# Hash bits on four column quarters, placed by way of DRAM, with three buffers for x

## The chip, the cores and the metric

One core of a Trainium2 chip. Its engines are TensorE (PE in the profile, PEld its weight loads), VectorE (DVE), ScalarE (ACT), GpSimd (POOL) and SyncE (SP). The metric is the device time of one execution in microseconds, as a median of several runs. All runs told here are of the fast state.

## The reference

Hash attention for 32 heads, followed by a feed-forward block:

```python
q_bits = (np.einsum('bhsd,dk->bhsk', q, proj) > 0)      # 6 bits a query, the same for keys
q_bucket = np.sum(q_bits * powers, axis=-1)
mask = q_bucket[:, :, :, None] == k_bucket[:, :, None, :]
scores = np.where(mask, scale * q @ k.T, -1e9)
attn = softmax(scores); x = attn @ v                     # 4 x 8 heads, 768 tokens, 64 wide
h = x @ w_in                                             # 3072 tokens, 512 -> 2048
out = (h * erf(softplus(h))) @ w_out
```

## The kernel before

The heads go in 16 pairs, the two heads of a pair (a, b) on partitions 0 to 63 and 64 to 127. The mask comes from a matmul of hash bits (qb, kb; values of plus and minus one, the keys weighted by 2^100) that is added to the score matmul in the same bank. The hash of a pair takes four matmuls of 64 columns, in two rounds, and one sign on ScalarE; VectorE then spreads the key bits of each head and doubles the query bits:

```python
def hash_bits(d, big, halves=(0, 1)):
    ...
    for half in halves:
        for n, what in enumerate("qk"):
            nc.tensor.matmul(out=d["bits"][n * D : n * D + D, half, 0:HS], lhsT=proj_sb,
                             rhs=d[what][:, half * HS : (half + 1) * HS], start=True, stop=True)
...
def spread_bits(d, cols, ab):      # twice a pair, 64 x 768
    nc.vector.tensor_scalar(out=d["kb"][ab * D : ab * D + D, cols], in0=d["qb"][D:P, cols],
                            scalar1=weight[D:P, ab : ab + 1], scalar2=None, op0=ALU.mult)
def double_bits(d, cols):          # once a pair, 64 x 768
    nc.vector.tensor_copy(out=d["qb"][D:P, cols], in_=d["qb"][0:D, cols])
```

The result of a pair (x) leaves its PSUM bank (the memory that TensorE writes into) by a ScalarE copy. The divisors (z) go to DRAM and back to be inverted, come back as r, VectorE normalises x and SyncE sends it to DRAM (xs). x has two buffers; z and r take turns in two others:

```python
def home(i, what):
    if i < NPAIR - 1:
        return xst.tile([P, S], F32, name=what, tag="x" if what == "x" else "z")   # bufs=2
```

A list scheduler orders all operations by assumed costs when the kernel is built; every engine then runs its own list strictly in order. TensorE's order is fixed by hand. With h counting half pairs:

```python
order += [("score", n) for n in (2 * h + 1, 2 * h + 2) if n < NS]
if h % 2 == 0 and h // 2 + 1 < NPAIR:
    order.append(("bits", h // 2 + 1))
if h >= 1:
    order.append(("divisor", h - 1))
order += [("weigh", 2 * h), ("weigh", 2 * h + 1)]     # the av groups of the profile
...
op(start_pair, (i,), "SP", 3.6, (0, n - 6),            # loads q, k, v of pair i
   (("weigh", n - 9), ("bits_of", i - 1)) + ..., late=3.5)
```

## Time and profile before

| | before |
|---|---|
| time, median of 4 runs | 933.61 us |
| attention with setup, in the profiled run | 339.4 us |
| feed-forward part | 593.5 us |
| one pair of heads, undisturbed | 20.32 us |
| busy in such a period: PE, VectorE, ScalarE | 20.32, 19.64, 15.86 us |
| PE stalls over 14 pairs | 4.3 us |

The first two stretches and the period are shown in the prediction. In this program the useful yardstick is the start of each av group (24 passes, once per half pair): the distances between them show every stall, which the share of busy time does not, because PE is marked busy nearly throughout. I call the 32 groups av 0 to av 31.

### The profile page before, as it was taken

Reading aid. Unit: us, or ns where it says so; the run is one execution under the profiler, and the core shown is the slowest. Engines: PE = TensorE matmul, PEld = TensorE weight load, DVE = VectorE, ACT = ScalarE, POOL = GpSimd, SP = SyncE. Lnnn points to the kernel's source line nnn. Section 1 sums busy time; section 2 is a strip of 40 time slices with the busy share of each in tenths; the row PEclk is TensorE's granted clock in tenths of the full one; section 3 lists DMA queues with packets and bytes.
Section 4 is the critical chain, followed back from the end, with each engine's and each line's share of the span. In section 5 each row is a group of like instructions: output and inputs, shape, how many; then the busy total and the mean of one; then the engine's idle time right before and its main releaser. Section 6 shows DMA issues by size and latency. Waiting matters only on the chain.

```text
span 932.9 us, 12993 instructions
## 1 busy us (share of the span) xinstructions
PE 916.8 (98%) x5003; PEld 661.9 (71%) x5003; DVE 829.7 (89%) x1041; ACT 771.0 (83%) x1002; POOL 17.4 (2%) x35
## 2 busy tenths in 40 slices
PE   8999999999999999999999999999999999999996
PEld 3444444444444458888888888888888888888885
DVE  4999998999888997899999889998899789988995
ACT  5888787768876838999998998899989997899891
POOL 0000000000000000000000000000000000000000
PEclk9999999999999999999999999999999999999998
DMA  8365455576654322010212012210221111001211
GB/s 198 99 158 147 132 148 139 147 200 165 147 149 131 97 103 97 1 46 34 80 68 79 34 46 69 80 34 34 79 78 36 34 65 49 34 34 46 68 35 48
DMA packets 61398, 80.92 MB, mean 87 GB/s; under 512 B 33296, under 2 KB 46224, under 8 KB 61328
## 3 DMA queue, kind: packets, MB, share of 16 engines
q1 hardware_dynamic: 56672, 64.08, 23.9%
q0 software_dynamic: 4352, 15.73, 5.6%
q8 instruction: 41, 0.67, 0.3%
q10 hardware_dynamic: 304, 0.20, 0.1%
q14 instruction: 29, 0.24, 0.1%
HBM read 64.07 MB, written 15.93 MB: 86 GB/s over the span
## 4 chain that ended last, share of the span: by engine, by line
PE 85%; DVE 7%; DMA 4%; ACT 2%; issue 1%; SPq 0%; DVEq 0%; ACTq 0%
PE M L1238 30%; PE X L1098 27%; PE st L529 11%; PE av L602 9%; PE M L1098 3%; PE bits L358 2%; DMA xs<-x 1%; ACT e_all L543 1%; DVE x_sum L590 1%; PE z_ps L635 1%; DVE x L590 1%; DMA zd<-z 1%; DMA zc<-zd 1%; DVE x L721 1%; DMA r<-rd 1%
## 5 line engine op out<-in xcount | busy, mean ns | idle before, releaser
L1165 DVE SCALAR_TENSOR_TENSOR e<-w,e 128x1024 f32<-128x1024 f32 x144 | 173.4, 1221 | 5.8 <-ACT w L1161 3.0
L1161 ACT ACTIVATE w<-w,cq 128x1024 f32<-128x1024 f32 x144 | 160.7, 1143 | 1.9
L543 ACT ACTIVATE e_all<-st 128x768 f32<-128x768 f32 x192 | 149.1, 819 | 11.3 <-PE st L529 11.3
L529 PE MATMUL st<-q,k 64*128 64x384 f32 x768 | 156.6, 486 | 0.0
L1238 PE MATMUL M<-w_out_sb,h 128*128 128x256 f32 x576 | 140.2, 380 | 0.4 <-DVE h L1180 0.4
L602 PE MATMUL av<-e_all,v 128*64 128x385 f32 (+1 forms) x768 | 131.1, 490 | 0.0
L1098 PE MATMUL X<-x,w_in_sb 128*128 128x256 f32 x512 | 121.2, 380 | 0.0
L1238 PEld LDWEIGHTS M<-w_out_sb,h 128*128 128x128 f32 x576 | 109.3, 190 | 15.9 <-DVE h L1180 1.1
L1098 PEld LDWEIGHTS X<-x,w_in_sb 128*128 128x128 f32 x512 | 97.1, 190 | 13.8 <-ACT h L1116 0.6
L602 PEld LDWEIGHTS av<-e_all,v 128*64 128x64 f32 x768 | 52.4, 136 | 67.2 <-issue 65.4
L1238 PE MATMUL M<-wt,S 128*128 128x256 f32 x384 | 93.4, 379 | 0.4 <-DVE S L1195 0.4
L529 PEld LDWEIGHTS st<-q,k 64*128 64x128 f32 x768 | 69.1, 190 | 32.8 <-issue 32.1
L1098 PE MATMUL X<-x_sum,w_sum 128*128 128x256 f32 x344 | 81.7, 380 | 1.8 <-ACT h L1116 1.8
L1238 PEld LDWEIGHTS M<-wt,S 128*128 128x128 f32 x384 | 72.9, 190 | 10.7 <-DVE S L1195 0.8
L1098 PEld LDWEIGHTS X<-x_sum,w_sum 128*128 128x128 f32 x344 | 65.1, 190 | 12.0 <-ACT h L1116 3.3
L1116 ACT COPY h<-X 128x512 f32<-128x512 f32 x85 | 49.0, 577 | 22.3 <-PE X L1098 21.4
L1142 DVE SCALAR_TENSOR_TENSOR w<-w,e 128x1024 f32<-128x1024 f32 x48 | 58.4, 1221 | 9.6 <-ACT w L1137 9.3
L529 PE MATMUL st<-qb,kb 64*128 64x384 bf16 x384 | 63.7, 327 | 3.3 <-ACT e_all L543 3.2
L1180 DVE TENSOR_TENSOR h<-h,e 128x1024 f32<-128x1024 f32 x48 | 58.0, 1221 | 6.1 <-ACT e L1176 5.9
L659 ACT COPY x<-av 128x384 f32<-128x384 f32 x32 | 15.3, 478 | 57.4 <-DMA xs<-x 28.8
L1156 ACT ACTIVATE w<-e 128x1024 f32<-128x1024 f32 x48 | 50.4, 1050 | 13.3 <-DVE e L1152 13.0
L1152 DVE TENSOR_TENSOR e<-e,w 128x1024 f32<-128x1024 f32 x48 | 57.5, 1219 | 2.7 <-ACT e L1148 2.6
(117 smaller groups left out, 1421.0 us busy)
## 6 DMA issues: line engine op xcount, KB each, us to landing
wt<-wt SPq DMA_DIRECT2D x24, 768.0 KB, 4.3
raw<-in_w_out_dram POOLq DMA_DIRECT2D x16, 512.0 KB, 3.9
raw<-in_w_in_dram POOLq DMA_DIRECT2D x14, 512.0 KB, 4.2
v<-in_v_dram SPq DMA_DIRECT2D x32, 192.0 KB, 4.5
xs<-x SPq DMA_DIRECT2D x16, 384.0 KB, 2.4
q<-in_qkT_dram SPq DMA_DIRECT2D x30, 192.0 KB, 3.4
k<-in_qkT_dram SPq DMA_DIRECT2D x30, 192.0 KB, 4.2
r<-rd SPq DMA_DIRECT2D x30, 192.0 KB, 3.5
```

Source lines behind the costliest of these rows:

```text
L529: nc.tensor.matmul(out=st[:, ab, 0:HS], lhsT=d["k" + src][rows, keys], rhs=d["q" + src][rows, cols], start=(part == 0), stop=(part == 1),)
L543: nc.scalar.activation(out=e[:, :, 0:HS], in_=st[:, :, 0:HS], func=AF.Exp, scale=scale)
L602: nc.tensor.matmul(out=d["av"][rows, 0:w], lhsT=d["v"][:, g * GC + c, rows], rhs=e[:, ab, 0:w], start=(g == 0 and c == 0), stop=(g == 1 an ...
L1098: nc.tensor.matmul(out=d[where][:, u, :], lhsT=a[:, kc, f : f + P], rhs=b[:, kc, :], start=(first and u == 0 and kc == 0), stop=(last and ...
L1116: nc.scalar.copy(out=quarter(p, q), in_=st[p][where])
L1142: nc.vector.scalar_tensor_tensor(out=w, in0=w, scalar=-1.0, in1=st[p]["e", v], op0=ALU.add, op1=ALU.subtract)
L1152: nc.vector.tensor_tensor(out=s, in0=s, in1=st[p].pop(("w", v)), op=ALU.subtract)
L1156: nc.scalar.activation(out=z, in_=st[p]["s", v], func=AF.Square)
L1161: nc.scalar.activation(out=q, in_=z, func=AF.Square, bias=cq[:, j : j + 1])
L1165: nc.vector.scalar_tensor_tensor(out=s, in0=st[p].pop(("q", v, j)), scalar=ERF_Q[j][1], in1=s, op0=ALU.add, op1=ALU.mult,)
L1180: nc.vector.tensor_tensor(out=h, in0=h, in1=st[p].pop(("s", v)), op=ALU.mult)
L1238: nc.tensor.matmul(out=banks[name][:, sub, :], lhsT=a[:, u, sub * P : (sub + 1) * P], rhs=b[:, u, :], start=(c == 0 and k == 0), stop=(c = ...
```

## The change

It means to shorten the hash on TensorE by putting its four parts side by side on four column quarters. The bits then lie in other rows than the mask matmul reads. VectorE could move them, in eight instructions a pair (dve_place below); here GpSimd writes them to DRAM and reads them back into place: one write, two reads. VectorE keeps one spread of 64x384. As this takes longer, the hash of a pair moves half a pair earlier in TensorE's order (pair 1 stays). Further, x gets three buffers, z one of its own and r two; the last two sums move into other tiles to make room.

```diff
+                for n, what in enumerate("qk"):
+                    for half in range(2):
+                        row = (2 * n + half) * QR
+                        nc.tensor.matmul(out=d["bits"][row : row + QR, 0, 0:HS], lhsT=proj_q,
+                            rhs=d[what][:, half * HS : (half + 1) * HS], start=True, stop=True)
...
+            def leave_bits(i):
+                bd = pairs[i]["bd"] = dram.tile([4, 2, QB, HS], BF16, name="bd", tag="bd")
+                nc.gpsimd.dma_start(out=bd.rearrange("n a r c -> (n a r) c"), in_=sg)
+            def place_bits(i):
...
+                for ab in range(2):
+                    nc.gpsimd.dma_start(
+                        out=both[i % 2][ab * D : ab * D + NBIT + 1, :, :].rearrange(
+                            "r w (h c) -> r (w h) c", h=2),
+                        in_=bd[:, ab, 0 : NBIT + 1, :].rearrange("n r c -> r n c"))
...
-                if h % 2 == 0 and h // 2 + 1 < NPAIR:
-                    order.append(("bits", h // 2 + 1))
+                if h == 0:
+                    order.insert(3, ("bits", 1))
+                if h % 2 and (h + 3) // 2 < NPAIR:
+                    order.append(("bits", (h + 3) // 2))
...
-                    return xst.tile([P, S], F32, name=what, tag="x" if what == "x" else "z")
+                    shape, bufs = {"x": (S, 3), "z": (HS, 1), "r": (S, 2)}[what]
+                    return xst.tile([P, shape], F32, name=what, tag=what, bufs=bufs)
```

(Cut: the constants for the quarters, the clearing of the bit tiles, the new homes of the last sums, and the scheduler's dependencies and costs.)

More of the change, by code (lines that the diff above doesn't have):

```diff
@@ L230 @@
     QR = 32
+    QB = QR // 2
     WARM = 7
@@ L233 @@
     weight = const.tile([P, 2], F32, name="weight")
+    proj_q = const.tile([P, QR], F32, name="proj_q")
+    weight_q = const.tile([P, 1], F32, name="weight_q")
     ones = const.tile([P, D], F32, name="ones")
@@ L257 @@
     nc.gpsimd.dma_start(out=row, in_=bucket)
-    steps = const.tile([P, 5], F32, name="steps")
+    steps = const.tile([P, 8], F32, name="steps")
     for c, (end, factor) in enumerate(
@@ L265 @@
             (QR + NBIT + 1, -float(NBIT)),
+            (QB, -1.0),
+            (QB + NBIT, NBIT + 1.0),
+            (QB + NBIT + 1, -float(NBIT)),
         )
@@ L277 @@
     nc.vector.reduce_sum(out=weight[:, 1:2], in_=steps[:, 2:5], axis=AX.X)
+    nc.vector.memset(proj_q, 0.0)
+    for ab in range(2):
+        rows = slice(ab * D, ab * D + D)
+        nc.vector.tensor_copy(
+            out=proj_q[rows, ab * QB : ab * QB + NBIT],
+            in_=proj_in[rows, ab * NBIT : (ab + 1) * NBIT],
+        )
+    nc.vector.reduce_sum(out=weight_q, in_=steps[:, 5:8], axis=AX.X)
+    nc.vector.tensor_tensor(out=weight_q, in0=weight_q, in1=weight[:, 0:1], op=ALU.add)
+    nc.vector.tensor_copy(out=weight_q[D + QR : P, :], in_=weight_q[D : D + QR, :])
     nc.vector.memset(sgn, -(2.0**-27))
@@ L364, in hash_bits, with sign_bits @@
                 )
-    def sign_bits(d, bitp, cols):
+    def sign_bits(d, tile_of, cols):
         if cols.start == 0:
             for what in ("qb", "kb"):
-                d[what] = bitp.tile([P, S], BF16, name=what, tag=what)
+                d[what] = tile_of(what)
         nc.scalar.activation(
@@ L392, in double_bits, with take_bits @@
         nc.vector.tensor_copy(out=d["qb"][D:P, cols], in_=d["qb"][0:D, cols])
-    def take_bits(d, bitp, halves=(0, 1)):
+    def take_bits(d, tile_of, halves=(0, 1)):
         cols = slice(halves[0] * HS, (halves[-1] + 1) * HS)
-        sign_bits(d, bitp, cols)
+        sign_bits(d, tile_of, cols)
         for ab in (1, 0):
@@ L404, in attention @@
             tc.tile_pool(name="load", bufs=3) as load,
-            tc.tile_pool(name="bitp", bufs=2) as bitp,
+            tc.tile_pool(name="bitp", bufs=1) as bitp,
             tc.tile_pool(name="ep", bufs=1) as ep,
-            tc.tile_pool(name="sums", bufs=2) as sums,
-            tc.tile_pool(name="xst", bufs=2) as xst,
+            tc.tile_pool(name="xst", bufs=1) as xst,
             tc.tile_pool(name="rawp", bufs=2) as rawp,
@@ L415, in big @@
                 return psum.tile([P, 2, 512], F32, name=name, tag="big", bufs=3)
+            sg = bitp.tile([P, HS], BF16, name="sg")
+            both = [bitp.tile([P, 2, S], BF16, name=f"both{n}") for n in range(2)]
+            nc.gpsimd.memset(both[1], 0.0)
             junk = ep.tile([P, HS], BF16, name="junk")
@@ L574, in sum_keys @@
                     if h >= NH - 2:
-                        d["sum", half] = sums.tile([P, 1, 2, HS], F32, name="sum", tag="sum")
+                        if half:
+                            room = blocks[1][:, :, :].rearrange("p k t -> p (k t)")[:, 0:S]
+                        else:
+                            room = load.tile([P, S], F32, name="q", tag="q")
+                        d["sum", half] = room.rearrange("p (n a c) -> p n a c", n=1, a=2)
                     else:
@@ L612, in home @@
                 if i < NPAIR - 1:
-                    return xst.tile([P, S], F32, name=what, tag="x" if what == "x" else "z")
+                    shape, bufs = {"x": (S, 3), "z": (HS, 1), "r": (S, 2)}[what]
+                    return xst.tile([P, shape], F32, name=what, tag=what, bufs=bufs)
                 rows = blocks[1][:, :, :].rearrange("p k t -> p (k t)")
-                return rows[:, S : 2 * S] if what == "x" else rows[:, 0:S]
+                c = {"x": S, "z": 2 * S, "r": 0}[what]
+                return rows[:, c : c + (HS if what == "z" else S)]
             def measure(i, n, half):
@@ L757, in attention @@
                 hash_bits(pairs[0], big, (half,))
-                take_bits(pairs[0], bitp, (half,))
+                take_bits(pairs[0], lambda what: both[0][:, "qk".index(what[0]), :], (half,))
             NH = NPAIR * 2
@@ L773, in bits_of, with weigh_bits, clean @@
             def bits_of(i):
-                hash_bits(pairs[i], big)
-            def sign_of(i):
-                sign_bits(pairs[i], bitp, slice(0, S))
-            def weigh_bits(i, ab):
-                spread_bits(pairs[i], slice(0, S), ab)
-            def copy_bits(i):
-                double_bits(pairs[i], slice(0, S))
+                d = pairs[i]
+                d["bits"] = big("bits")
+                for n, what in enumerate("qk"):
+                    for half in range(2):
+                        row = (2 * n + half) * QR
+                        nc.tensor.matmul(
+                            out=d["bits"][row : row + QR, 0, 0:HS],
+                            lhsT=proj_q,
+                            rhs=d[what][:, half * HS : (half + 1) * HS],
+                            start=True,
+                            stop=True,
+                        )
+            def sign_of(i):
+                nc.scalar.activation(
+                    out=sg,
+                    in_=pairs[i].pop("bits")[:, 0, 0:HS],
+                    func=AF.Sign,
+                    scale=2.0**100,
+                    bias=sgn[:, 0:1],
+                )
+            def weigh_bits(i):
+                nc.vector.tensor_scalar(
+                    out=sg[D:P, :],
+                    in0=sg[D:P, :],
+                    scalar1=weight_q[D:P, 0:1],
+                    scalar2=None,
+                    op0=ALU.mult,
+                )
+            def leave_bits(i):
+                bd = pairs[i]["bd"] = dram.tile([4, 2, QB, HS], BF16, name="bd", tag="bd")
+                nc.gpsimd.dma_start(out=bd.rearrange("n a r c -> (n a r) c"), in_=sg)
+            def place_bits(i):
+                d = pairs[i]
+                bd = d.pop("bd")
+                for n, what in enumerate(("qb", "kb")):
+                    d[what] = both[i % 2][:, n, :]
+                for ab in range(2):
+                    nc.gpsimd.dma_start(
+                        out=both[i % 2][ab * D : ab * D + NBIT + 1, :, :].rearrange(
+                            "r w (h c) -> r (w h) c", h=2
+                        ),
+                        in_=bd[:, ab, 0 : NBIT + 1, :].rearrange("n r c -> r n c"),
+                    )
+            def clean():
+                nc.gpsimd.memset(both[0], 0.0)
             chain = []
@@ L797, in attention @@
                     i = n // 4
-                    after = tuple(("weigh_bits", i, ab) for ab in range(2)) + (("copy_bits", i),)
+                    after = (("place_bits", i),)
                     for c in range(GC):
@@ L803, in attention @@
                 elif what == "bits":
-                    pe(bits_of, (n,), 1.34, (("start_pair", n), slots[-3]))
+                    pe(bits_of, (n,), 0.92, (("start_pair", n), slots[-3]))
                     slots.append(("sign_of", n))
@@ L837, in attention @@
                         after += (("divisor", h - 2),)
+                        if h == NH - 2:
+                            after += (("measure", NPAIR - 3, 0, 1),)
                     op(sum_keys, (h, k), "DVE", 1.72 if where == 2 else 0.92, (1, 2 * h + 1, k), after)
@@ L846, in attention @@
                     (0, 2 * h, -1),
-                    (("divisor", h), ("send", i - 1) if i == NPAIR - 1 else ("widen", i - 1)),
+                    (("divisor", h), ("spread", i - 1)),
                 )
@@ L866, in attention @@
                     )
-                    op(sign_of, (i,), "ACT", 0.88, (0, n - 2, 9), (("bits_of", i), ("score", n - 5, 2)))
-                    for ab in (1, 0):
-                        op(weigh_bits, (i, ab), "DVE", 0.43, (0, n - 2, 1), (("sign_of", i),))
+                    op(sign_of, (i,), "ACT", 0.6, (0, n - 6, 9), (("bits_of", i), ("leave_bits", i - 1)))
+                    op(weigh_bits, (i,), "DVE", 0.33, (0, n - 6, 1), (("sign_of", i),))
+                    op(leave_bits, (i,), "POOL", 0.7, (0, n - 6, 2), (("weigh_bits", i),), late=2.6)
                     op(
-                        copy_bits,
+                        place_bits,
                         (i,),
-                        "DVE",
-                        0.35,
-                        (0, n - 2, 2),
-                        (("weigh_bits", i, 0), ("weigh_bits", i, 1)),
+                        "POOL",
+                        1.2,
+                        (0, n - 6, 3),
+                        (("leave_bits", i), ("score", n - 5, 2)) + (("clean",),) * (i == 2),
+                        late=2.6,
                     )
@@ L899, in attention @@
                     (0, n, 3),
-                    (("ungather", i), ("send", i - 1)),
+                    (("ungather", i), ("normalise", i - 2)),
                     late=6.5,
@@ L904, in attention @@
                 op(send, (i,), "SP", 0.35, (0, n, 4), (("normalise", i),), late=2.2)
+            op(clean, (), "POOL", 1.4, (0, 0), (("score", 3, 2),), late=0.3)
             for n in range(len(pieces)):
@@ L973, in general @@
                 hash_bits(d, big)
-                take_bits(d, bitp)
+                take_bits(d, lambda what: bitp.tile([P, S], BF16, name=what, tag=what))
                 x = ep.tile([P, S], F32, name="x", tag="x")
```

## The prediction

> **What bounds the kernel now.** I read the page's engine line and the 40 slices first, then a three-stretch table of busy time, then the chain of waits, then the timeline of the attention stretch.
>
> ```profile
> PE 916.8 (98%) x5003; PEld 661.9 (71%) x5003; DVE 829.7 (89%) x1041; ACT 771.0 (83%) x1002; POOL 17.4 (2%) x35
> ...
> PE 85%; DVE 7%; DMA 4%; ACT 2%; issue 1%; SPq 0%; DVEq 0%; ACTq 0%
> ```
> The first line says TensorE (PE) is nearly always occupied, the second that 85% of the chain that ended last is its work. A busy PE is not proof of a PE bound, so I asked how the time splits:
>
> ```profile
> 9.60:339.40 329.80, 325.96 (x2290) 150.69 (x2289) 300.17 (x419) 256.07 (x463) 16.55 (x30) 1.00 0.54 142
> 339.40:932.90 593.50, 583.63 (x2700) 509.86 (x2700) 527.06 (x602) 513.03 (x538) 0.00 (x0) 1.00 0.16 55
> ```
> Columns: length, then busy us of PE, PEld, DVE, ACT, POOL, then clock, DMA share, GB/s. Attention takes 330 us, the feed-forward part 594 us. The change edits attention and its setup only, so I expect the 594 us to stay, and everything is decided in the first stretch. There one pair of heads repeats every 20.32 us (the z_ps group at 101 us to the av group at 121.66 us, below). What PE does at the end of such a period:
>
> ```profile
> 119.02 0.81 PE L529 MATMUL st<-q,k 64*128 64x384 f32 x4
> 119.76 0.54 PE L358 MATMUL bits<-q,proj_sb 128*64 128x384 f32 x1
> 119.76 0.54 PE L358 MATMUL bits<-k,proj_sb 128*64 128x384 f32 x1
> 120.13 0.49 PE L358 MATMUL bits<-q,proj_sb 128*64 128x384 f32 x1
> ...
> 121.20 0.53 PE L635 MATMUL z_ps<-x,ones 128*32 128x192 f32 x8
> 121.66 3.78 PE L602 MATMUL av<-e_all,v 128*64 128x385 f32 x22
> ```
> Columns: start, duration, engine, line, names, shape. Every fp32 matmul shows as two passes. Start to start is the cost, since the ends overlap. A q pass and a k pass start together (they sit on two column halves of the array) and the next two come 0.32 us later: four steps of 0.32 plus 0.16 of changeover, 1.44 us for the hash bits. The divisor (z_ps) puts four 32-column matmuls on four column quarters, and all eight passes of 192 columns take 0.46 us: two steps of 0.16 plus 0.14. Four quarters do run side by side here.
>
> PE is not quite gapless. From the av group at 29.56 us to that at 318.32 us in the chain are 14 pairs, 288.76 us; 14 x 20.32 = 284.48. So 4.3 us are stalls. Where:
>
> ```profile
> 286.97 0.73 ACT L460 ACTIVATE keep<-keep,tiny 128x512 int32<-128x512 f32 x1
> 293.69 0.48 ACT L659 COPY x<-av 128x384 f32<-128x384 f32 x1 [5.99 <-DMA xs<-x]
> 294.07 2.22 ACT L543 ACTIVATE e_all<-st 128x768 f32<-128x768 f32 x3
> ```
> ```profile
> 292.14 0.81 PE L529 MATMUL st<-q,k 64*128 64x384 f32 x4
> 294.94 0.34 PE L529 MATMUL st<-qb,kb 64*128 64x384 bf16 x2 [1.99 <-ACT e_all L543]
> ```
> ScalarE wants to empty the av bank into x, whose buffer is still being sent out; it sits 5.99 us, its exponentials behind it come late, and PE waits 1.99 us for a score bank. The table of waits has this kind seven times, 28.8 us of ACT time, longest 6.0.
>
> **What the Trainium skill says.** "TensorEngine Tiling (Array Packing)", section "Key Properties": tiles execute in parallel, and changing the tiling mode drains the array; section "Available Configurations" lists 128x32 as four tiles. The trace agrees: four at once, and some 0.10 to 0.16 us at each change of shape. "DMA: Bandwidth & Descriptors", section "Anatomy of one DMA": a GpSimd-issued transfer costs about 2.0 us plus bytes/436e3, mostly the receipt of the last byte. The trace's only small one, the 0.5 KB row load, landed in 2.9 us; the 512 KB weight loads took 3.9 to 4.2. The same page, "Rules for kernel authors": a transfer that reads what another wrote must wait for its semaphore, so the trip by way of DRAM costs two landings in a row. "SBUF — State Buffer", section "Who interferes with whom": GpSimd and a VectorE operation in a two-port mode lock each other out. In this trace 30 GpSimd issues beside a VectorE that is over 90% busy took 0.53 to 0.77 us, so I expect no starvation.
>
> **The change part by part.**
> 1. Hash matmuls: four of 64 columns in two rounds become four of 32 columns in one round. Two steps of 0.32 plus 0.16 is 0.80 us, or 0.70 if the changeover to the divisor, which now has the same tiling, disappears. Saved: 0.64 to 0.74 us, on the PE path, for 15 pairs (pair 0 keeps the old way). I take 0.69: **-10.4 us**.
> 2. VectorE loses two spreads of 0.419 and a copy of 0.354 (1.19 us a pair), and gains one 64x384 spread of 0.318: -0.87 us a pair. ScalarE's sign shrinks from 0.901 (128x768) to 0.580 (128x384): -0.32. Both lie beside PE, so no direct gain; but VectorE is busy 19.64 of 20.32 us in the period from 101.41 to 121.73 us, and without this relief a PE period of 19.63 us would just meet it. With it, VectorE needs 18.8.
> 3. Three x buffers: the copy out of the av bank waits for a send one pair older, which in the trace ended some 20 us earlier than the one waited for; the longest wait is 6. All seven waits should go. I count most of the stalls as recovered: **-3.6 of 4.3 us**.
> 4. Own divisor buffer: z and r took turns in two buffers, so z already waited only for its own spread. Two for r let the broadcast come earlier. Worth nothing directly.
> 5. The DRAM trip: sign 0.6, spread 0.3, write 0.7 to issue and in all about 2.9 to land, two reads of about 0.7 and then 2.9: roughly 9 us with queueing. From pair 2 on the bits are computed half a pair earlier, and between them and the first score that needs them lie two av groups (8.06), two divisors (0.9) and nine scores (7.4): 16 us. Hidden. Pair 1 cannot be moved earlier: between its bits (end about 19.5 us) and its first score lie one av group (4.03) and three scores (2.43), so PE is there at 25.9. The chain is sign to 20.9, spread to 21.3, write landed 24.2, reads issued to 25.6, landed about 27.9. A stall once: **+2.0 us**.
> 6. Setup: some ten small VectorE instructions of 0.06 to 0.17 us and two GpSimd memsets. VectorE's setup ended at 4.80 us, PE's first hash matmul came at 5.78 behind the warm-up: **+0.3 us** at most.
>
> Sum: -10.4 - 3.6 + 2.0 + 0.3 = -11.7; 933.7 becomes 922.0.
>
> **Rivals.**
> - The trip takes the place of the removed work: GpSimd's queue is in order and its weight loads wait for free buffers (up to 25 us in the table of waits). If a load that waits for VectorE stands ahead of the placing, PE stalls in many pairs. Against: 16 us of slack against 9, and the loads fire about once per half pair, just before the hash. If wrong, 1 to 2 us in half of the pairs: 930 to 936.
> - The inputs come too late: hash bits half a pair earlier need q and k 10 us earlier, and the SyncE queue issues them behind a send that waits for VectorE. In the old trace such a load was issued at 268.68 us, behind the send at 268.27. Against: the load's place in the queue followed the previous pair's hash, which moves forward too. If it stays behind the sends, up to 1 us a pair comes back: 925 to 932.
> - ACT or DVE becomes the bound at 19.63 us a pair: DVE would be at 95%, as now (97%), so bursts might cost some of part 1: 925.
> - No overlap of the quarters: gain of part 1 gone, 932. The divisor speaks against it.
> - Everything recovers and pair 1 has no stall: 918.
>
> **Range and chances.** The terms of part 1 are seen in the trace, to within 1.5 us in sum; the stalls and pair 1 are good to 2 us each; the rivals mostly push up. Range 917.5 to 928. Over 2% faster would need below 915, more than all savings together allow; 2% slower needs a new stall in every pair.
>
> **What would show it.** Hash groups of 128*32 shape, 120 passes, start to start about 0.7 us from bits to z_ps; a period of about 19.6 us; no ACT copy of x that waits for xs<-x; one PE wait for placed bits near 26 us and none later; the feed-forward stretch within 1 us of 593.5. Repeated PE waits on GpSimd's transfers, or hash matmuls that wait for q or k, would prove me wrong.

## The result, and the profile after

| | before | after |
|---|---|---|
| median | 933.61 us (931.88 to 935.03, 4 runs) | 920.59 us (918.86 to 923.69, 4 runs) |
| ratio of the fast runs | | 0.9865, 95% interval 0.9832 to 0.9899 |

A ratio here is the mean time of one kernel's fast runs over that of the other's in the same rounds, so it is not quite the ratio of the medians. The change saves 13.0 us by the medians, 1.35% by the ratio: within 2%.

The page of the kernel after, its engine line and the first line of its chain of waits:

```profile
PE 904.2 (99%) x5003; PEld 657.1 (72%) x5003; DVE 820.2 (89%) x1020; ACT 768.2 (84%) x1002; POOL 46.1 (5%) x82
...
PE 95%; DVE 2%; ACT 1%; DMA 1%; issue 0%; POOL 0%; DVEq 0%; POOLq 0%
```

PE is busy 12.6 us less with the same 5003 passes, and its share of the chain has gone from 85% to 95%: the DMA and VectorE pieces of the chain, 11% together before, are 3%. The two long stretches, in the columns told in the prediction:

```profile
9.60:325.10 315.50, 313.38 (x2289) 146.03 (x2288) 289.95 (x391) 253.46 (x463) 43.85 (x76) 1.00 0.59 156
325.10:917.70 592.60, 583.64 (x2700) 509.71 (x2700) 526.18 (x600) 512.92 (x537) 0.00 (x0) 1.00 0.16 54
```

The attention stretch is 14.3 us shorter, the feed-forward part 0.9. The end of a period on PE, in the timeline:

```profile
107.50 0.81 PE L547 MATMUL st<-q,k 64*128 64x384 f32 x4
108.24 0.52 PE L805 MATMUL bits<-q,proj_q 128*32 128x384 f32 x2
108.25 0.52 PE L805 MATMUL bits<-k,proj_q 128*32 128x384 f32 x2
108.59 0.49 PE L805 MATMUL bits<-q,proj_q 128*32 128x384 f32 x2
108.60 0.49 PE L805 MATMUL bits<-k,proj_q 128*32 128x384 f32 x2
108.91 0.51 PE L659 MATMUL z_ps<-x_sum,ones 128*32 128x192 f32 x8
109.35 4.09 PE L624 MATMUL av<-e_all,v 128*64 128x384 f32 x24
```

Four passes start within 0.01 us of each other and the next four about 0.33 us later. From the first hash pass to the divisor it is 0.67 us where it was 1.44. The period is 19.53 us in place of 20.32.

The two profiled runs, cut at the starts of the av groups:

| piece | before | after | difference |
|---|---|---|---|
| start to av 0 | 20.09 | 18.90 | -1.19 |
| av 0 to av 1 | 9.39 | 11.56 | +2.17 |
| av 1 to av 29 | 288.77 | 273.54 | -15.23 |
| av 29 to the first feed-forward matmul | 21.13 | 21.13 | 0.00 |
| from there to the end | 593.52 | 592.57 | -0.95 |
| whole span | 932.90 | 917.70 | -15.20 |

Four later runs with the new hash order have no stall between av 1 and av 29 and take 272.77 us there; two of them have none between av 0 and av 1 and take 10.09 us. With these I split the 15.2 us:

- the shorter hash: 0.56 for pair 1 (1.34 to 0.78 us up to av 0), and (284.48 - 272.77) - (10.09 - 9.39) = 11.0 for the rest, in all **-11.6 us**;
- stalls between av 1 and av 29: from 288.77 - 284.48 = 4.3 to 273.54 - 272.77 = 0.8, **-3.5 us**;
- a new stall between av 0 and av 1: 11.56 - 10.09, **+1.5 us**;
- start and end: -0.6 and -0.95 us, which I do not ascribe to the change. The start is told below; the end varies by such an amount between all the runs here.

The profiled run of before (934.86 us) was 1.2 us above its median and that of after (919.47 us) 1.1 below, which is why the traces differ by more than the medians.

The new stall, in the timeline of the kernel after (all engines, the rows that concern pair 1):

```profile
19.10 0.60 ACT L814 ACTIVATE sg<-bits,sgn 128x384 bf16<-128x384 f32 x1
...
19.74 0.32 DVE L824 TENSOR_SCALAR sg<-sg,weight_q 64x384 bf16<-64x384 bf16 x1
...
20.36 0.55 POOL L834 DMA_DIRECT2D bd<-sg  x1 [17.05 <-DVE sg L824]
...
24.05 1.14 POOL L843 DMA_DIRECT2D both<-bd  x2 [3.14 <-DMA bd<-sg]
...
26.27 0.32 PE L547 MATMUL st<-both 64*128 64x384 bf16 x1 [0.74 <-DMA both<-bd]
...
26.83 0.33 PE L547 MATMUL st<-both 64*128 64x384 bf16 x1 [0.24 <-DMA both<-bd]
```

This is the chain of the prediction: sign, spread, write, wait for the write, two reads, and PE waits for each of the two. The stall of 0.8 us between av 1 and av 29 is of another kind, at 66 us:

```profile
64.08 0.69 ACT L471 ACTIVATE keep<-raw 128x512 f32<-128x512 f32 x1 [3.98 <-DMA raw<-in_w_in_dram]
...
66.65 0.34 PE L547 MATMUL st<-both 64*128 64x384 bf16 x2 [0.59 <-ACT e_all L561]
```

GpSimd's weight load came late, behind a placing (GpSimd had sat 4.18 us before the placing at 56.98 us), ScalarE waited for the weights with the exponentials behind it, and PE ran out of score banks.

### The profile page after: what moved, and what is told of

The parts are those of the page before. It is cut to its first block, busy times and chain, and to the rows that moved or that the text cites. A ratio compares the mean times of both kernels' runs of the same rounds, so it can differ in the third digit from the quotient of the medians.

```text
span 917.7 us, 13114 instructions
## 1 busy us (share of the span) xinstructions
PE 904.2 (99%) x5003; PEld 657.1 (72%) x5003; DVE 820.2 (89%) x1020; ACT 768.2 (84%) x1002; POOL 46.1 (5%) x82
## 4 chain that ended last, share of the span: by engine, by line
PE 95%; DVE 2%; ACT 1%; DMA 1%; issue 0%; POOL 0%; DVEq 0%; POOLq 0%
PE M L1313 31%; PE X L1173 28%; PE st L547 16%; PE av L624 14%; PE M L1173 3%; PE z_ps L659 1%; PE bits L805 1%; ACT e_all L561 1%; PE warm L773 0%; DVE e L1227 0%; PE bits L374 0%; DMA bd<-sg 0%; DVE h L1255 0%; DMA both<-bd 0%; DVE S L1270 0%
## 5 line engine op out<-in xcount | busy, mean ns | idle before, releaser
L561 ACT ACTIVATE e_all<-st 128x768 f32<-128x768 f32 x192 | 151.5, 813 | 14.2 <-PE st L547 12.8
L547 PE MATMUL st<-both 64*128 64x384 bf16 x384 | 63.7, 326 | 1.6 <-DMA both<-bd 1.0
L1195 DVE TENSOR_TENSOR h<-X,h 128x512 f32<-128x512 f32 x65 | 44.8, 689 | 16.4 <-PE X L1173 15.4
```

What stands on the lines that cost most here:

```text
L547: nc.tensor.matmul(out=st[:, ab, 0:HS], lhsT=d["k" + src][rows, keys], rhs=d["q" + src][rows, cols], start=(part == 0), stop=(part == 1),)
L561: nc.scalar.activation(out=e[:, :, 0:HS], in_=st[:, :, 0:HS], func=AF.Exp, scale=scale)
```

## The experiments

Theory A is that of the prediction: PE is the bound of attention, the hash gain is on its path in full, the third x buffer removes the stalls, the DRAM trip is hidden except for pair 1. Theory B, formed on reading the trace of after: the stalls went because the earlier hash lets the scheduler put a pair's input loads ahead of the send of x on SyncE. In the kernel before, SyncE does this (its timeline; SPq marks a transfer that SyncE issues):

```profile
81.95 0.33 SPq L727 DMA_DIRECT2D xs<-x  x1
82.37 1.13 SPq L342 DMA_DIRECT2D q<-in_qkT_dram  x2
83.55 1.23 SPq L342 DMA_DIRECT2D k<-in_qkT_dram  x2
84.82 1.17 SPq L347 DMA_DIRECT2D v<-in_v_dram  x2
86.09 0.58 SPq L678 DMA_DIRECT2D zd<-z  x1
```

and in the kernel after this:

```profile
94.19 1.18 SPq L358 DMA_DIRECT2D q<-in_qkT_dram  x2
95.42 1.23 SPq L358 DMA_DIRECT2D k<-in_qkT_dram  x2
96.74 1.12 SPq L363 DMA_DIRECT2D v<-in_v_dram  x2
98.88 0.34 SPq L751 DMA_DIRECT2D xs<-x  x1
99.74 0.59 SPq L702 DMA_DIRECT2D zd<-z  x1
```

Before, the send stands first and has waited for VectorE (so in all periods but one: the loads at 96.05 us stand ahead of their send), then come the loads, and only then the divisor's spread (zd), which the next send depends on: 5.1 us after the av group at 81.01 us. After, the loads stand in the time in which the send would wait anyway; in the period before the one shown, the spread was issued 0.5 us after av 6 at 79.73 us (at 80.21 us).

### two_x: the changed kernel with two x buffers

```diff
-                    shape, bufs = {"x": (S, 3), "z": (HS, 1), "r": (S, 2)}[what]
+                    shape, bufs = {"x": (S, 2), "z": (HS, 1), "r": (S, 2)}[what]
```

> The changed kernel with two x buffers in place of three, all else kept. Theory A (the one of the prediction: the third x buffer took the stalls away): the copies out of the av bank wait for the send again, some seven waits of up to 6 us on ScalarE, TensorE loses about 3.5 us, time about 924. Theory B (the hash half a pair earlier lets the input loads stand ahead of the sends in the SyncE queue, so the sends end earlier: in the changed trace a send is issued at 98.88 us and the copy that two buffers would hold back comes at 103.4): waits of under 1 us each, TensorE loses under 1 us, time 920 to 921.5.

Measured: 923.82 us (922.5 to 925.85, 4 runs), ratio 0.9909 to the kernel before. ScalarE waits for the send three times, 12.2 us in all. From av 1 to av 29 it is 275.35 us, so 2.6 us of stalls: between the two theories. The rest of its time is at the start, for another reason. Its scores were at full rate before 9.8 us (12.2 us in the trace of after), so the hash of pair 1 came 1.75 us earlier; its bits did not (the write took 4.6 us to land in place of 3.0, and the reads were issued at 23.99 us, against 24.05), so PE waited 3.6 us, and then ran slowly. Windows of this run, in the columns of before, the clock third from the right:

```profile
20.00:24.00 4.00, 3.78 (x26) 1.56 (x22) 2.60 (x6) 2.70 (x5) 0.01 (x1) 1.00 0.38 71
27.00:30.90 3.90, 3.44 (x13) 2.15 (x15) 1.47 (x2) 0.81 (x1) 0.02 (x1) 0.60 0.86 236
```

After the wait the granted clock is 0.60 in this window. From av 0 to av 1 it took 15.93 us in place of 10.09. The Trainium skill, "TensorE: Matmul & The Clock Gate", section "What's actually happening", has PE at half clock after an idle window of about 3.4 us and the windows free-running; the wait of 3.6 us and the varying start agree with both. The interval of this run's ratio (0.9873 to 0.9946) overlaps that of after (0.9832 to 0.9899), so what the missing buffer costs is read from the trace and not from the times.

### bufs_only: the kernel before with the buffers alone

```diff
-                    return xst.tile([P, S], F32, name=what, tag="x" if what == "x" else "z")
+                    shape, bufs = {"x": (S, 3), "z": (HS, 1), "r": (S, 2)}[what]
+                    return xst.tile([P, shape], F32, name=what, tag=what, bufs=bufs)
```

(and the new homes and dependencies of the last sums, z and r, as in the change)

> The kernel before with the buffers alone changed (three for x, an own one for z, two for r, no pool for the last sums) and the hash as it was. If a third x buffer cures the stalls by itself: no ScalarE wait for a send, 14 periods of 20.32 us without the 4.3 us of stalls, time about 930. If the buffers do nothing without the earlier hash: 933 to 934, with the waits still there.

Measured: 932.23 us (20 runs) beside 932.07, ratio 0.9996, interval 0.9982 to 1.001: no gain, and a time between the two that were expected. The waits for the send are gone, as theory A says, yet the stalls from av 1 to av 29 went only from 4.3 to 2.9 us (287.41 us). In its table of waits stands one in their place:

```profile
ACT z L653 <- DMA zd<-z: 5.7, 6, 1.8
```

ScalarE now waits for the z buffer to be read by its spread, which is late behind the loads, and in places PE waits for the key bits from VectorE. One wait was replaced by the next in the same chain.

### loads_first: the kernel before with the loads ahead of the send

```diff
-                        (("weigh", n - 9), ("bits_of", i - 1))
+                        (("weigh", n - 9),)
```

This touches only what the scheduler believes about the loads; real dependencies are kept.

> The kernel before, old hash and two x buffers, only that on SyncE the input loads of a pair stand ahead of the send of x in place of behind it (the order that the changed kernel got from its earlier hash). Theory B: the loads then fill the time in which the send waits for VectorE, the divisor's spread is issued right after the send, some 4 us earlier, and the sends come 3 to 4 us earlier: ScalarE's waits for a send fall from 28.8 us to under 10, the stalls of TensorE over 14 pairs from 4.3 to under 2 us, time 929 to 931.5 against 932 to 933.6. If the buffer count decides: waits and stalls as before, 932 to 934.

Measured: 930.03 us (22 runs) beside 931.36, ratio 0.9984, interval 0.9974 to 0.9993. The wait for the send, in the table of waits of the kernel before, and then in that of this run (total, times, longest):

```profile
ACT x L659 <- DMA xs<-x: 28.8, 7, 6.0
...
ACT x L659 <- DMA xs<-x: 9.7, 3, 3.5
```

The stalls from av 1 to av 29 are 285.27 - 284.48 = 0.8 us, with two buffers and the old hash. So in this trace the kernel whose loads stand ahead of the send is nearly free of the stalls that I had put down to the want of a third buffer. The gain by the median, 1.3 us, is less than the 3.5 us between the traces; the profiled run of before may have had more stalls than a usual one, which I have not shown. The scheduler also moved operations of VectorE and ScalarE in this kernel (TensorE's and GpSimd's lists are the same), so the isolation is not perfect.

### hash_twice: the hash matmuls made twice

```diff
-                for n, what in enumerate("qk"):
-                    for half in range(2):
+                for n, what, half in [(n, w, h) for _ in range(2) for n, w in enumerate("qk") for h in range(2)]:
+                    if True:
```

> The changed kernel with the hash matmuls of pairs 1 to 15 made twice, the second over the first (the same result). If the four-quarter hash lies on the path at its full length: two more steps of 0.32 to 0.33 us a pair, a period of 20.18 us in place of 19.53, 15 times 0.65 is 9.8 us more, about 930.4. If TensorE has slack that hides it: under 3 us more.

Measured: 928.45 us (20 runs), 7.9 more than after; the period is 20.17 us, so 0.64 us more a pair. The hash lies on the path in full. That the sum is 7.9 and not 15 times 0.64 = 9.6 us fits its first groups: av 0 to av 1 took 10.95 us, less than the 12.2 that the doubled hash and the stall of pair 1 would add up to, since the longer PE work may hide part of the wait; the wait also differs between executions (0.7 us in after_again, 1.5 in after).

### more_dve: VectorE gets its relief back

```diff
+                for _ in range(3):
+                    nc.vector.tensor_scalar(
+                        out=idle, in0=idle, scalar1=1.0, scalar2=None, op0=ALU.mult
+                    )
```

> The changed kernel with three idle VectorE instructions of 64x384 bf16 after each pair's spread, some 0.96 us a pair, about what the change took from VectorE (0.87). If VectorE's relief is needed for the period of 19.53 us (18.8 busy now, 19.7 then): a period of about 19.7 us and stalls, 2 to 8 us more, 923 to 929. If the relief is worth nothing on the path: within 1 us of 920.6.

Measured: 924.34 us (922.75 to 925.18, 4 runs), ratio 0.9909: 3.8 us more than after, though the intervals of the ratios (0.9878 to 0.994, 0.9832 to 0.9899) overlap. The period without stalls stays 19.53 us, but there are 276.37 - 272.77 = 3.6 us of them, most in one kind of its table of waits:

```profile
PE av L626 <- DVE ev L691: 2.9, 4, 1.3
```

PE waits for a tiny VectorE instruction that frees the av bank and stands behind other work in VectorE's list. VectorE's share of the chain that ended last is 14% on this run's page and 2% on that of after. So the 0.87 us a pair taken from VectorE is worth some 4 us on the path, by one trace, although the period without stalls does not show it.

### dve_place: VectorE places the bits, no DRAM

```diff
-                nc.vector.tensor_scalar(out=sg[D:P, :], in0=sg[D:P, :], scalar1=weight_q[D:P, 0:1], ...)
+                for half in range(2):
+                    for ab in range(2):
+                        nc.vector.tensor_copy(out=d["qb"][rows, cols], in_=sg[half * QR : (half + 1) * QR, :])
+                        nc.vector.tensor_scalar(out=d["kb"][rows, cols], in0=sg[at : at + QR, :],
+                            scalar1=weight_w[at : at + QR, ab : ab + 1], scalar2=None, op0=ALU.mult)
```

(rows of 32 with zero weights for the other head; the three transfers removed)

> The changed kernel with the bits placed by VectorE in place of the trip by way of DRAM: eight instructions of 32x384 bf16 a pair in place of one of 64x384. Each about 0.25 to 0.32 us, 2.3 us a pair in place of 0.32, so VectorE needs 18.8 + 2.0 = 20.8 us a pair. If VectorE then bounds the pair: a period of 20.5 to 21 us, 933 to 942. If TensorE stays the bound because VectorE's low-rank weight work slips into the feed-forward stretch: 921 to 925.

Measured: 938.93 us (7 runs), ratio 1.0066: 18.3 us more than after, in the range of the first theory. The mechanism is both at once: 282.40 - 272.77 = 9.6 us of stalls from av 1 to av 29 (20.17 us a pair, less than the 20.5 expected), and a wait of 8.1 us in the first feed-forward tile, for VectorE work that had been pushed back (timeline):

```profile
345.31 6.22 PE L1163 MATMUL M<-x_sum,w_sum 128*128 128x256 f32 x16 [8.08 <-DVE x_sum L349]
```

This is what the trip by way of DRAM buys.

### late_bits: the hash back at its old place

```diff
-                if h == 0:
-                    order.insert(3, ("bits", 1))
-                if h % 2 and (h + 3) // 2 < NPAIR:
-                    order.append(("bits", (h + 3) // 2))
+                if h % 2 == 0 and h // 2 + 1 < NPAIR:
+                    order.append(("bits", h // 2 + 1))
```

> The changed kernel with the hash of pair i back at its old place in TensorE's order, half a pair later. Between the hash and the first score that needs it there are then about 6.5 us in place of 16 to 17. If the trip of about 15 us that the changed trace shows (hash at 108.24 us, placed at about 124 us) is what the earlier place hides: TensorE stalls in every pair, by 3 us if the trip shrinks to 9 as the prediction had it, by 8 if it stays at 15: 45 to 120 us more, 965 to 1040. If the trip is short when it is urgent: under 15 us more.

Measured: 943.11 and 951.33 us, two runs that lie 8 us apart (ratio 1.0151, interval 1.0086 to 1.0216), some 27 us more than after; from av 1 to av 29 it is 298.51 us in the first, so about 1.8 us of stall a pair. Both numbers of the expectation missed. The kind of wait is the expected one (15.1 of the 25.7 us as the table counts them, by ends of matmuls that are modelled):

```profile
PE st L547 <- DMA both<-bd: 15.1, 20, 3.0
```

The trip is shorter here than in the kernel after. There VectorE takes the spread 4.1 us after the hash (median of 15) and the reads are issued 9.1 us after it (4.9 to 13.9); here it is 2.4 and about 6 us. The scheduler orders VectorE by what it believes urgent, so the trip of after had spent part of its slack in VectorE's list. The landings are shorter too: 2.3 us for a write and 2.1 for a read in the median, against 3.4 and 4.0 in after. From the hash to the landing of the second read it is 8.8 us in the median here and 14.2 in after. One read of each, first after (landed in 4.9 us) and then this run (2.1 us), in the columns of before, the DMA share second from the right:

```profile
96.97:101.91 4.94, 4.94 (x40) 2.17 (x38) 4.80 (x5) 3.94 (x7) 1.72 (x3) 1.00 1.16 224
...
106.67:108.82 2.15, 2.15 (x16) 0.90 (x12) 2.08 (x5) 1.71 (x3) 1.81 (x4) 1.00 0.07 20
```

VectorE is busy in both lines; what differs is the share of the DMA engines that other transfers keep busy (it can pass 1 where packets overlap). In after the reads fall beside the loads that SyncE issues, in this run mostly not.

### sync_trip: the transfers issued from SyncE

```diff
-                nc.gpsimd.dma_start(out=bd.rearrange("n a r c -> (n a r) c"), in_=sg)
+                nc.sync.dma_start(out=bd.rearrange("n a r c -> (n a r) c"), in_=sg)
```

(the two reads likewise, and the engine of both operations in the scheduler)

> The changed kernel with the three transfers of a pair issued from SyncE in place of GpSimd. Landings should be shorter (the old trace has 1.4 to 2.4 us for small SyncE transfers against 3.4 and 4.0 for these), so the stall of pair 1 should shrink from 1.5 to about 0.5 us. Against it, the queue is in order and already holds loads, sends and the divisor's trip: if these get in each other's way, sends or loads come late and TensorE stalls: 922 to 930. If not: 919.5.

Measured: 940.32 us (934.79 to 943.06, 13 runs), ratio 1.0066, worse than both theories had it. From av 1 to av 29 it is 292.73 us. PE waits six times for k to be loaded (2.9 us) and six times for VectorE's av instruction (6.6 us). I read this as one queue that carries too many waits, which no further run tested; on GpSimd's queue only weight loads stand beside the three transfers.

### early_first: the hash of pair 1 one score group earlier

```diff
-                    order.insert(3, ("bits", 1))
+                    order.insert(2, ("bits", 1))
```

> The changed kernel with the hash of pair 1 one score group earlier (before the third group in place of after it), 2.4 us more for its trip. Theory: the one stall at 26 us goes, from the first av group to the second it takes about 10.05 us in place of 11.56, time 1.5 us lower, about 919. Rival: the inputs of pair 1 are not there yet or the score banks run short, and TensorE waits before the hash in place of after it: no gain.

Measured: 918.75 us (918.42 to 919.32, 4 runs), ratio 0.9854 (0.9821 to 0.9886), which does not part it from after. PE's wait moved forward, as the rival said: 0.7 us before av 0 for the score bank that the sign had not freed, since three of ScalarE's squares stood ahead of the sign. From av 0 to av 1 it is still 10.85 us.

### after_again, first_here, first_here_two_x: pair 1 placed by VectorE

after_again is the changed kernel unaltered. first_here gives pair 1 the eight VectorE instructions of dve_place and clears its tile before pair 3 uses it; first_here_two_x has two x buffers besides.

```diff
-                    after = (("place_bits", i),)
+                    after = (("place_bits" if i != 1 else "place_here", i),)
...
-                        (("leave_bits", i), ("score", n - 5, 2)) + (("clean",),) * (i == 2),
+                        (("leave_bits", i), ("score", n - 5, 2)) + (("clean", i % 2),) * (i in (2, 3)),
```

(place_here is the loop shown under dve_place; first_here_two_x adds the edit of two_x)

> The changed kernel once more, to stand beside the next two on one chip. 919 to 923; its runs should differ by about 2 us among themselves, because the moment when the first matmuls come to full speed differs between executions (at about 13.4 us in the trace of before, 12.2 in that of after, before 9.8 in two_x).

> The changed kernel, only that the bits of pair 1 are placed by VectorE (eight instructions of 32x384, once) and not by way of DRAM. Theory: the trip of pair 1 is the one stall that the change added; without it the time from the first av group to the second is about 10.1 us in place of 11.56 (15.93 in two_x, where TensorE was at full speed earlier, waited 3.6 us and then ran slowly for a while): 1.5 to 4 us less than after_again, 917 to 919.5. Rival: the stall comes back at pair 2 or 3, whose placing now waits for one more memset: no gain.

> first_here with two x buffers. If the third buffer matters also with the earlier hash: ScalarE waits for a send again (3 times, 12.2 us in two_x), TensorE loses 2 to 3 us after the second av group, so 2 to 3 us more than first_here. If the stalls of two_x were its slow start alone: the same as first_here.

| | median | runs | ratio to before | av 0 to av 1 | av 1 to av 29 |
|---|---|---|---|---|---|
| after_again | 920.39 us | 918.2 to 921.21 | 0.9871 | 10.77 | 272.77 |
| first_here | 918.12 us | 917.52 to 919.22 | 0.9846 | 10.09 | 272.77 |
| first_here_two_x | 919.83 us | 919.6 to 920.25 | 0.9863 | 10.09 | 272.77 |

The runs of after_again lie 3.0 us apart, where about 2 were expected. first_here has no PE stall left up to av 31 and the lowest median, by 2.3 us against after_again on the same chip; with 5 and 4 runs the intervals of the ratios (0.9826 to 0.9865, 0.9847 to 0.9894) still overlap. With two x buffers ScalarE waits for a send once, 2.5 us, and PE does not stall at all in the profiled run. Its runs are nevertheless 1.7 us slower than first_here's; the trace shows 0.7 of it before av 1 and 1.4 us after the attention part, which the buffers do not explain. So the third buffer's own worth beside the earlier hash lies between 0 (this trace) and 2.6 us (two_x), by execution.

## Why the prediction was right

The time, 920.59 us, lies in the range, and the saving of 13.0 us is near the forecast 11.7. The signs that it named came true in the trace of after: a period of 19.53 us, 0.67 us from the bits to z_ps, no copy of x that waits for a send, waits for placed bits only near 26 us, a feed-forward stretch of 592.6 us. Two of its readings were loose: the step from the first hash passes to the next is 0.37 us in the lines shown and only the later ones are 0.32, and the 20.32 us run from one av group to another (101.34 to 121.66 us), not from a z_ps group. By its own steps:

1. **Hash matmuls.** Predicted 0.64 to 0.74 us a pair, measured 0.79 in the period. The mechanism was right and hash_twice shows it on the path in full; the term was undersized, 10.4 against 11.6 us. I had taken the middle between a new hash with a changeover (0.80 us) and one without (0.70); it takes 0.67 us, two steps of about 0.33 and nothing else.
2. **VectorE and ScalarE.** "No direct gain, but without it VectorE would just meet the period" held by and large: VectorE is busy 18.20 us in the period from 109.42 to 128.95 us (18.8 were expected), and more_dve lost 3.8 us when it got the work back.
3. **Three x buffers.** Here the size was right by luck and the cause that I gave was only a part. Predicted -3.6 us, and 3.5 us of stalls are gone between the two traces (a usual run of before may have fewer, see loads_first); but bufs_only recovers nothing in time, with 2.9 us of stalls left, and loads_first has them at 0.8 us with two buffers. The step that failed is "all seven waits should go" taken as the recovery of the stalls: the waits went with the buffers, the stalls did not. The loads' place on SyncE, which I had brought up only as a danger, is the other part; each of the two shortens the same chain. How the 3.5 us divide between them in the kernel after is not settled: with the loads ahead, the third buffer was worth 2.6 us in the trace of two_x and nothing in that of first_here_two_x.
4. **Own divisor buffer.** "Worth nothing directly" stands; bufs_only shows that z waits for its own spread, as said.
5. **The DRAM trip.** Pair 1: predicted 2.0 us of stall, measured 1.5 in the trace of after, 0.7 in after_again and 5.8 in two_x (3.6 of waiting, the rest at the slower clock). It is a race between PE's warm-up and the arrival of the bits, not a constant: the hash began at 16.37 us in two_x and 18.12 in after, and the reads were issued at 23.99 and 24.05. "Cannot be moved earlier" was wrong as to the place in the order (early_first moved it), but the bits came no sooner for PE. For the later pairs "roughly 9 us with queueing" was mis-sized. The reads were issued 9.1 us after the hash in the median and 13.9 at worst, and the second read landed 14.2 us after it in the median and 16.6 at worst, with 17.0 of slack where I had 16. The two terms that were too small are the wait in VectorE's list (2.4 us between sign and spread in the median, 5.3 at worst) and the landings (3.4 and 4.0 us for 2.9); in late_bits, with a quieter DMA, the trip was 8.8 us. GpSimd was not starved, as expected: its 45 issues for the bits took 0.55 to 0.59 us each. The trip stayed hidden, with little to spare: the reads of pair 10, issued at 200.26 us, had to land for the scores at 203.5.
6. **Setup.** At most 0.3 us predicted; the first hash passes start at 5.78 us in both traces, so nothing.

Of the rivals, the trip of later pairs and the late loads cost nothing in the kernel after. The GpSimd queue did give back 0.8 us, in the opposite sense: a placing held up a weight load. sync_trip and late_bits show both dangers when the queue or the slack is taken away.

## What to carry to other kernels

When a buffer's wait shows up, look at what stands ahead of its releaser in the in-order queue before adding a buffer: a second wait in the same chain may be all that the buffer uncovers. Small stationary operands that sit on distinct column quarters ran side by side here, and neighbours of the same shape saved the changeover too (0.67 us for 1.44). A round trip by way of DRAM takes work off a crowded engine if it is started early, but its length depends on the list of the engine that feeds it and on the other transfers that are under way (8.8 to 14.2 us here), and the first trip of a program, which little hides, may be worth doing another way (2.3 us by the medians here).

## What the Trainium skill lacked or had wrong

- "DMA: Bandwidth & Descriptors", section "Anatomy of one DMA": its fit (about 2.0 us plus bytes/436e3) gives 2.2 us for the 96 KB write and 2.05 for a read of 21 KB. In the loaded kernel they took 1.9 to 5.7 us (median 3.4) and 2.1 to 5.1 (median 4.0). Where the DMA engines were quiet (late_bits) a read took 2.1 us in the median, as the fit has it. The fit has no term for other traffic on the engines.
- "TensorEngine Tiling (Array Packing)", section "Key Properties": it says that a change of the tiling mode drains the array but gives no cost. Here the hash took 1.44 us, four steps of 0.32 and 0.16 over, before a divisor of another tiling; with the same tiling as the divisor it took 0.67 us, two steps and 0.03.
- No page has what a list scheduler's order of in-order queues does to such waits: waits for a send of 28.8 us before and 9.7 with the loads ahead of the send, all buffers being the same.
